# Cached attention gated by an MLP: how the last head group's sums, query and output matmuls are laid out in time

## The chip, the cores and the metric

One core of a Trainium2 chip. The number is device time in microseconds (us) of one execution of the whole kernel, as a median of several runs. TensorE (PE in the profile) multiplies matrices, VectorE (DVE) and ScalarE (ACT) work on tiles, GpSimd is POOL, and SyncE (SP) issues nearly all DMAs, in the order of the program.

## The reference

The inputs are bf16: x of 2048 x 512, a K and a V cache of 32 heads x 2048 keys x 128, and weights.

```python
xn = _layernorm(x)
q  = (xn @ wq) per head                       # 32 heads of 128
p  = softmax(q @ k.T * 128 ** -0.5)           # 2048 x 2048 per head
s  = concat(p @ v) @ wo                       # 2048 x 512
x1 = xn + shift(gelu(_layernorm(xn) @ w1)) @ w2   # shift: four quarters moved by 1, -1, 2, -2 rows
b  = x1 + gelu(_layernorm(x1) @ w3) @ w4
out = x + s * silu(b)
```

## The kernel before, in words

The kernel first makes xn, its transpose xnT and most of the MLP branch ("the start", up to about 130 us). Then comes the main loop over 128 **units**. A unit is one head for one tile of 512 queries. The heads go in eight groups of four (HG = 4, L51), and the order is group, query tile, head of the group (L120), so a group is 16 units, and the last group is units 112 to 127. A unit has eight **slots** (SPU, L54). Each slot takes two chunks of 128 keys.

In a slot TensorE makes two score matmuls into a PSUM tile ps_s (`s_slot`, L280; two such tiles exist, L95). ACT turns the tile into exponentials pT (L291). Some slots later TensorE multiplies two chunks of pT with V into ps_o (`pv_slot`, L310; two PSUM tiles, L92). How many slots later is PV's **lag**. `pv_run` (L648) sets it: 5 for the first eight units, then growing to 10, and 10 until unit PV1, from where it falls by one a unit to 5. Where it falls, the first slot of a unit holds four PV matmuls instead of two.

The softmax denominators are the column sums of pT over all keys. DVE adds the eight slots of pT into one tile acc (`add_first` L297, `add_next` L302, `add_last` L302, L307, L308). What is left is a sum over the 128 partitions, and there are two ways:

- `sums(u)` (L320): four small matmuls of TensorE, acc against a column of ones, into ps_sum, then the reciprocal rc on DVE (L327).
- `turn(u)` and `turned_sums(u)` (L331 to L342): a DMA transpose of acc on SP into tT, then a reduction on DVE (L338) and the reciprocal (L340). Units in the range TURN (L124) go this way: now 12 to 107.

In both ways rc goes to DRAM by one DMA (dr, L329 or L342) and comes back to all partitions by another (rb, `bcast`, L346). `norm(u)` (L358, DVE) multiplies ps_o by rb into oT, and thereby frees the PSUM tile of ps_o two units on.

When the four heads of a query tile are normalised, `norm_queue` (L662) puts four tiles of 128 rows into the queue wo_todo. `wo_slot` (L672) takes one: four matmuls (`wo_mm`, one for each head) into ps_wo, PSUM tag xm with one buffer, and then `wo_post` (L400), which on DVE adds ps_wo to the sums sacc (L416) or, in the last two groups, applies gate and input (L409 and L412, L409 and L397, or L425 and L427) and issues the output on SP.

The query tile of a unit takes four matmuls (`q_mm`, L264) and a copy (`q_copy`, L272). Units in the list `made` are made ahead in the start by `q_ahead` (L514): PSUM tag xa for even, xm for odd units, one buffer each, and the copy on ACT (L277). These are now 0 to 8, 112 to 116, 126 and 127, the last four of the list in the order 8, 116, 126, 127. All others are made in the loop in the unit before, in tag xa, with the copy on DVE (L275); ps_sum uses xa too.

The order of the instructions on each engine is the program's (`pin`, L62), written out by hand in the loop at L689 to L727: for each slot the scores, PV, query matmuls, then by slot number the sums, the normalisation, the Wo matmuls and the additions. For turned units a slot gets one query matmul (slots 7, 0, 1, 2) or one Wo matmul (slots 3 to 6). For others two query matmuls (slots 0, 1) and two Wo matmuls (slots 4, 5) share a slot, the sums are in slot 4, the normalisation in slot 3 (`late`, L710). The last unit, 127, is written out at L733 to L752; its own denominators and output come in the lines after.

Of the kernel before, what the change touches and what calls it, by code (L numbers as in the profile page):

```python
# [17 lines left out]
def kernel(  # L18
# [32 lines left out]
    HG = 4  # L51
# [69 lines left out]
    LATE = (QT - 2, QT - 1)  # L121
    GY = NG - 2
    NU = len(units)
    TURN = range(3 * HG, NU - 5 * HG)  # L124
    PV0, PV1 = 2 * HG, NU - 5 * HG + 3
    NS = NU * SPU
    kTs, vBs, wqs, wos, oTs, st = {}, {}, {}, {}, {}, {}
    todo = defaultdict(list)
# [49 lines left out]
    def stats(src, mv, rs, t):  # L178
        bn = smp.tile([P, nc.vector.BN_STATS_DIM], FP32, name="bn")
        pin(nc.vector.bn_stats(out=bn[:], in_=src))  # L180
        pin(nc.vector.bn_aggr(out=mv[:, t, :], in_=bn[:]))
        rsqrt(rs[:, t:t + 1], mv[:, t, 1:2])
# [34 lines left out]
    def m2(t):  # L217
        ps = psO.tile([P, D], FP32, tag="ps_o", name="ps_o")
        for jc in range(DC):
            c0 = BASE_J[jc] + t * P - SHIFT[jc]  # L220
            mm(ps[:], hT[:, jc, c0:c0 + P], w2_sb[:, jc, :], jc == 0, jc == DC - 1)
        return ps

    def x1(t, ps):
        pin(nc.vector.tensor_tensor(out=xall[:, t, :], in0=ps[:], in1=xall[:, t, :], op=ALU.add))
# [38 lines left out]
    def q_mm(u, dcs, tag="xa"):  # L264
        g, qt, hh = units[u]
        if dcs[0] == 0:
            st[u] = dict(psq=psX.tile([P, 512], FP32, tag=tag, name="ps_q"))
        for dc in dcs:
            mm(st[u]["psq"][:], wqs[g * HG + hh][:, dc, :],
               xnT[:, dc, qt * 512:(qt + 1) * 512], dc == 0, dc == DC - 1)  # L270
# [29 lines left out]
    def add_next(u, i):  # L300
        a = st[u]["acc"]
        pin(nc.vector.tensor_tensor(out=a[:], in0=a[:], in1=st[u]["pT"][i][:], op=ALU.add))  # L302

    def add_last(u):
        add_next(u, 3)
        a = st[u]["acc"]
        pin(nc.vector.tensor_tensor(out=a[:, 0:2, :], in0=a[:, 0:2, :], in1=a[:, 2:4, :], op=ALU.add))  # L307
        pin(nc.vector.tensor_tensor(out=a[:, 0, :], in0=a[:, 0, :], in1=a[:, 1, :], op=ALU.add))  # L308
# [40 lines left out]
    def norm(u):  # L349
        g, qt, hh = units[u]  # L350
        s = st.pop(u)
        if hh == 0:
            oTs[(g, qt)] = pB.tile([P, HG, 512], BF16, tag="oT", bufs=2, name="oT")
        o, rb, to = s["o"][:], s["rb"][:], oTs[(g, qt)][:, hh, :]
        if u in TURN:
            o = o.rearrange("k (j p) -> k p j", j=4)
            rb, to = (x.rearrange("k (p j) -> k p j", j=4) for x in (rb, to))
        pin(nc.vector.tensor_tensor(out=to, in0=o, in1=rb, op=ALU.mult))  # L358

    wo_box = {}  # L360
# [6 lines left out]
    def o_cols(g, qt, hh, ts):  # L367
        o = oTs[(g, qt)][:, hh, :]
        if (g * QT + qt) * HG + hh in TURN:
            return o.rearrange("k (p j) -> k j p", j=4)[:, ts, :]  # L370
        return o[:, ts * P:(ts + 1) * P]

    def wo_mm(g, t, hhs):
        if hhs[0] == 0:
            wo_box[0] = psX.tile([P, D], FP32, tag="xm", name="ps_wo")
        ts = t % 4
        for hh in hhs:
            mm(wo_box[0][:], o_cols(g, t // 4, hh, ts), wos[g * HG + hh][:], hh == 0, hh == HG - 1)
# [3 lines left out]
    def fin_load(t):  # L382
        xl = tokp.tile([P, D], BF16, tag="ta", bufs=10, name="xl")
        pin(nc.sync.dma_start(out=xl[:], in_=xsrc[t]))
        fin[t] = xl
# [14 lines left out]
    def wo_post(g, t, n):  # L400
        ps = wo_box.pop(0)
        if g == 0:
            sacc[t] = pS.tile([P, D], FP32, tag="sacc", bufs=NT, name="sacc")
            pin(nc.vector.tensor_copy(out=sacc[t][:], in_=ps[:]))
            return
        sa, gl = sacc[t][:], xall[:, t, :]
        if t // 4 in LATE and g >= GY:
            tm = pS.tile([P, D], FP32, tag="tm", bufs=4, name="tm")
            pin(nc.vector.scalar_tensor_tensor(  # L409
                out=tm[:], in0=ps[:], scalar=0.5, in1=gl, op0=ALU.mult, op1=ALU.mult))  # L410
            if g < NG - 1:
                pin(nc.vector.tensor_tensor(out=sa, in0=sa, in1=tm[:], op=ALU.add))  # L412
            else:
                y_out(t, tm, nc.sync)
            return
        pin(nc.vector.tensor_tensor(out=sa, in0=ps[:], in1=sa, op=ALU.add))  # L416
        if t // 4 in LATE and g == GY - 1:
            k = n + SPU * (t - 4 * LATE[0]) + 1
            at(max(k - SPU, n + 1), lambda: fin_load(t))
            at(k, lambda: y_scale(t))  # L420
            at(k + SPU, lambda: y_add(t))
        if g < NG - 1:
            return
        xl = fin.pop(t)
        pin(nc.vector.scalar_tensor_tensor(  # L425
            out=gl, in0=sa, scalar=0.5, in1=gl, op0=ALU.mult, op1=ALU.mult))
        pin(nc.vector.tensor_tensor(out=xl[:], in0=gl, in1=xl[:], op=ALU.add))  # L427
        pin(nc.sync.dma_start(out=out2d[t * P:(t + 1) * P, :], in_=xl[:]))
# [83 lines left out]
    made = []  # L512

    def q_ahead(u):  # L514
        q_mm(u, range(DC), ("xa", "xm")[u % 2])
        q_copy(u, nc.scalar)
        made.append(u)
# [24 lines left out]
        x1(t, ps)  # L542
    for t in range(4):
        stats(xall[:, t, :], mv2, rs2, t)
    for u in range(NU - 4 * HG, NU - 3 * HG):
        q_ahead(u)
    for t in range(4, 8):
        x1(t, m2(t))
# [2 lines left out]
    m1(1536, 512)  # L551
    for t in range(8, 11):
        x1(t, m2(t))
    for u in (2 * HG, NU - 12, NU - 2, NU - 1):
        q_ahead(u)
    for t in range(4, 8):
        stats(xall[:, t, :], mv2, rs2, t)
# [43 lines left out]
    pS = None  # L601
# [43 lines left out]
    wo_todo = deque()  # L645
# [16 lines left out]
    def norm_queue(u):  # L662
        norm(u)
        gg, qq, hh = units[u]
        if hh == HG - 1:
            wo_todo.extend((gg, 4 * qq + ts) for ts in range(4))
            if gg == NG - 1 and qq not in LATE:
                fin_load(4 * qq)

    UA, UB = NU - 2, NU - 1  # L670

    def wo_slot(part, n, each=2):  # L672
        gg, t = wo_todo[0]
        if part < HG // each:
            wo_mm(gg, t, tuple(range(part * each, (part + 1) * each)))
            return
        wo_todo.popleft()
        wo_post(gg, t, n)
        if gg == NG - 1 and t % 4 < 3 and t + 1 not in fin and t // 4 not in LATE:
            fin_load(t + 1)  # L680

    q_plan = defaultdict(list)
    for v in range(1, NU):
        if v not in made:
            for dc in range(DC):
                k = dc - 1 if v - 2 in TURN else dc // 2
                q_plan[(v - 1) * SPU + k].append((v, (dc,)))

    for n in range(UB * SPU):  # L689
        u, p = divmod(n, SPU)  # L690
        extra = len(wo_todo) > 3 and u < 2 * HG + 2 and pS is not None or u >= UA - 1
        s_slot(u, p)
        pv_run(n)
        for v, dcs in q_plan.get(n, ()):
            q_mm(v, dcs)
        if p == 0 and u - 2 in TURN:
            turned_sums(u - 2)
        if p == 1 and u - 2 in TURN:
            bcast(u - 2)
        if p == 0 and 1 <= u:  # L700
            add_last(u - 1)
        if p == 3 and u - 1 in TURN:
            turn(u - 1)
        if p == 0:
            twice = extra
        if twice and p < 3:
            wo_slot(p, n)
        if p == (3 if u - 1 in TURN else 2) and u + 1 not in made:
            q_copy(u + 1)
        late = 0 if u <= NU - 5 * HG else 2 if u <= NU - 5 * HG + 2 else 1  # L710
        if p == (7 if u - 2 in TURN else 2 + late) and 2 <= u:
            norm_queue(u - 2)
        if p == 3 + late and 1 <= u and u - 1 not in TURN:
            sums(u - 1)
        if p == 4 + late and 1 <= u and u - 1 not in TURN:
            bcast(u - 1)
        each, p0 = (1, 3) if u - 2 in TURN else (2, 4)
        if p0 <= p <= p0 + HG // each and wo_todo and pS is not None:
            wo_slot(p - p0, n, each=each)
        if p == 4:  # L720
            add_first(u)
        if p == 6:
            add_next(u, 2)
        held_mm(n)
        for fn in todo.pop(n, ()):
            fn()
        if n == HELD * SPU - 1:  # L727
            right.close()
            pS = right.enter_context(pool("pS", side="right", reuse_waits="tile"))
# [3 lines left out]
    n = UB * SPU  # L733
    ident2 = pS.tile([P, P], BF16, tag="ident2", name="ident2")
    pin(nc.vector.tensor_scalar(out=ident2[:], in0=ident[:], scalar1=2.0, scalar2=None, op0=ALU.mult))
    for p in range(SPU):
        s_slot(UB, p)
        pv_run(n + p)
        if p == 0:
            add_last(UA)  # L740
        if p < 2:
            wo_slot(p, n + p)
        if p == 3:
            norm(UB - 2)
            sums(UA)
            wo_slot(2, n + p)
        if p == 4:
            bcast(UA)
            add_first(UB)
        if p == 6:  # L750
            add_next(UB, 2)
# [90 lines left out]
```

## Time and profile before

| | |
|---|---|
| median of 3 runs | 1257.75 us (1257.68 to 1257.93) |
| profiled execution | 1258.32 us, its span 1256.5 |
| TensorE, large matmuls, start to start | 0.2158 us |
| units 96 to 107 (turned sums) | 8.63 us each |
| units 111 to 115 (sums by matmul, queries made ahead) | 8.39 to 8.40 |
| units 116 to 124 (sums by matmul, queries in the loop) | 8.80 each |
| unit 125, 126 (two Wo tiles each) | 9.02, 8.80 |
| exp of one slot (L291) on ACT | 1.02 us |
| last output landed | 1255.4 |

The span is what the profile shows of one execution, from its first to its last instruction. Durations are those of single instructions; an engine's next instruction can start before the end of the last, so a sum over a queue goes by the distances between starts. A unit's length is the distance between its first kT weight load and the next unit's.

### The profile page before, as it was taken

Reading aid. Unit: us, or ns where it says so; the run is one execution under the profiler, and the core shown is the slowest. Engines: PE = TensorE matmul, PEld = TensorE weight load, DVE = VectorE, ACT = ScalarE, POOL = GpSimd, SP = SyncE. Lnnn points to the kernel's source line nnn. Section 1 sums busy time; section 2 is a strip of 40 time slices with the busy share of each in tenths; the row PEclk is TensorE's granted clock in tenths of the full one; section 3 lists DMA queues with packets and bytes.
Section 4 is the critical chain, followed back from the end, with each engine's and each line's share of the span. In section 5 each row is a group of like instructions: output and inputs, shape, how many; then the busy total and the mean of one; then the engine's idle time right before and its main releaser. Section 6 shows DMA issues by size and latency. Waiting matters only on the chain.

```text
span 1256.5 us, 16202 instructions
## 1 busy us (share of the span) xinstructions
PE 1238.1 (99%) x5782; PEld 604.2 (48%) x5899; DVE 997.1 (79%) x1430; ACT 1100.6 (88%) x1113; POOL 34.4 (3%) x91
## 2 busy tenths in 40 slices
PE   8999999999999999999999999999999999999997
PEld 4444444444444444444444444444444444444443
DVE  7621567788888888888888888888888989978887
ACT  4344889999999999999999999999999999998886
POOL 4330000000000000000000000000000000000000
PEclk9999999999999999999999999999999999999999
DMA  6493011344345424454344514453355444452222
GB/s 157 104 167 77 10 32 46 79 91 96 58 74 108 107 51 75 97 102 84 60 89 98 110 42 86 87 118 68 56 101 104 100 67 84 97 94 51 68 56 59
DMA packets 224945, 103.86 MB, mean 83 GB/s; under 512 B 176928, under 2 KB 208160, under 8 KB 224864
## 3 DMA queue, kind: packets, MB, share of 16 engines
q1 hardware_dynamic: 221648, 100.07, 39.5%
q0 software_dynamic: 672, 1.84, 0.9%
q10 hardware_dynamic: 2544, 0.92, 0.3%
q8 instruction: 46, 0.75, 0.3%
q14 instruction: 35, 0.29, 0.1%
HBM read 67.90 MB, written 2.36 MB: 56 GB/s over the span
## 4 chain that ended last, share of the span: by engine, by line
PE 95%; DVE 2%; DMA 1%; ACT 1%; issue 1%; POOL 0%; SPq 0%; DVEq 0%; ACTq 0%
PE ps_s L109 39%; PE ps_o L109 36%; PE ps_q L109 9%; PE ps_wo L109 9%; PE ps_m L109 2%; DVE acc L302 0%; PE ps_sum L109 0%; ACT qT L277 0%; ACT xnT L199 0%; DMA rb<-dr 0%; DMA wq_e<-in_A_wq_dram 0%; DMA dr<-rc 0%; PE ps_w L109 0%; DMA xin<-in_A_x_dram 0%; DVE xall L425 0%
## 5 line engine op out<-in xcount | busy, mean ns | idle before, releaser
L291 ACT ACTIVATE pT<-ps_s 128x1024 bf16<-128x1024 f32 x1024 | 1034.6, 1023 | 76.0 <-PE ps_s L109 28.1
L109 PE MATMUL ps_s<-qT,kT 128*128 128x512 bf16 x2041 | 607.6, 379 | 0.6
L109 PE MATMUL ps_o<-pT,vb 128*128 128x512 bf16 x1962 | 589.0, 379 | 0.5
L302 DVE TENSOR_TENSOR acc<-acc,pT 128x2048 bf16<-128x2048 bf16 x255 | 309.3, 1213 | 98.2 <-ACT pT L291 95.7
L109 PEld LDWEIGHTS <-kT 128*128 128x128 bf16 x2048 | 231.1, 113 | 219.8 <-issue 0.8
L109 PEld LDWEIGHTS <-vb 128*128 128x128 bf16 x2048 | 200.3, 98 | 226.4 <-issue 0.3
L109 PE MATMUL ps_wo<-wo_h,oT 128*128 128x512 bf16 x492 | 177.9, 379 | 2.1
L297 DVE TENSOR_TENSOR acc<-pT 128x2048 bf16<-128x2048 bf16 x128 | 156.0, 1219 | 29.3 <-ACT pT L291 28.8
L109 PE MATMUL ps_q<-xnT,wq_h 128*128 128x512 bf16 x481 | 172.7, 379 | 2.1
L358 DVE TENSOR_TENSOR oT<-ps_o,rb 128x512 bf16<-128x512 f32 x127 | 86.9, 685 | 14.9 <-DMA rb<-dr 13.0
L307 DVE TENSOR_TENSOR acc<-acc 128x1024 bf16<-128x1024 bf16 x127 | 87.9, 692 | 4.3
L109 PEld LDWEIGHTS <-oT 128*128 128x128 bf16 x508 | 54.6, 110 | 56.6 <-DVE oT L358 1.2
L275 DVE CAST qT<-ps_q 128x512 bf16<-128x512 f32 x112 | 76.3, 682 | 0.3 <-PE ps_q L109 0.3
L109 PEld LDWEIGHTS <-wq_h 128*128 128x128 bf16 x484 | 47.2, 98 | 56.1 <-issue 0.2
L416 DVE TENSOR_TENSOR sacc<-ps_wo,sacc 128x512 f32<-128x512 f32 x96 | 65.5, 682 | 3.2 <-PE ps_wo L109 2.7
L338 DVE TENSOR_REDUCE sm<-tT 128x4 f32<-128x512 bf16 x96 | 64.9, 676 | 1.2 <-DMA tT<-acc 1.2
L308 DVE TENSOR_TENSOR acc<-acc 128x512 bf16<-128x512 bf16 x127 | 53.9, 425 | 4.3
L242 ACT ACTIVATE h2T<-ps_s 128x1024 bf16<-128x1024 f32 x28 | 28.7, 1024 | 24.0 <-PE ps_s L109 24.0
L109 PE MATMUL ps_s<-xn2T,w_sb 128*128 128x512 bf16 x219 | 48.6, 379 | 0.3
L109 PEld LDWEIGHTS <-w_sb 128*128 128x128 bf16 x304 | 29.7, 98 | 34.6 <-issue 2.1
L109 PEld LDWEIGHTS <-h2T 128*128 128x128 bf16 x224 | 21.5, 98 | 25.0 <-issue 0.2
L109 PE MATMUL ps_m<-w_sb,h2T 128*128 128x512 bf16 x106 | 31.0, 379 | 0.5
(73 smaller groups left out, 332.4 us busy)
## 6 DMA issues: line engine op xcount, KB each, us to landing
rb<-dr SPq DMA_DIRECT2D x127, 256.0 KB, 4.1
vb<-in_A_v_cache_dram SPq DMA_DIRECT2D x64, 256.0 KB, 3.2
wo_h<-in_A_wo_dram SPq DMA_DIRECT2D x32, 128.0 KB, 3.7
wq_h<-in_A_wq_dram SPq DMA_DIRECT2D x28, 128.0 KB, 3.2
w_sb<-in_B_w_dram SPq DMA_DIRECT2D x9, 256.0 KB, 4.8
kT<-in_A_k_cache_dram SPq DMA_TRANSPOSE x128, 3.2
xl<-in_A_x_dram SPq DMA_DIRECT2D x16, 128.0 KB, 3.6
dr<-rc SPq DMA_DIRECT2D x127, 2.0 KB, 1.4
```

Source lines behind the costliest of these rows:

```text
L109: pin(nc.tensor.matmul(out=out, lhsT=lhsT, rhs=rhs, start=start, stop=stop))
L242: pin(nc.scalar.activation(out=h2[c, f][:], in_=ps[:], func=ACT.Gelu_apprx_tanh))
L275: pin(nc.vector.tensor_copy(out=qT[:], in_=st[u].pop("psq")[:]))
L291: pin(nc.scalar.activation(out=s["pT"][-1][:, jj:jj + 2, :], in_=sps[:], func=ACT.Exp, scale=SCALE))
L297: pin(nc.vector.tensor_tensor(out=s["acc"][:], in0=s["pT"][0][:], in1=s["pT"][1][:], op=ALU.add))
L302: pin(nc.vector.tensor_tensor(out=a[:], in0=a[:], in1=st[u]["pT"][i][:], op=ALU.add))
L307: pin(nc.vector.tensor_tensor(out=a[:, 0:2, :], in0=a[:, 0:2, :], in1=a[:, 2:4, :], op=ALU.add))
L308: pin(nc.vector.tensor_tensor(out=a[:, 0, :], in0=a[:, 0, :], in1=a[:, 1, :], op=ALU.add))
L338: pin(nc.vector.tensor_reduce(out=sm[:], in_=s["tT"][:], axis=mybir.AxisListType.X, op=ALU.add))
L358: pin(nc.vector.tensor_tensor(out=to, in0=o, in1=rb, op=ALU.mult))
L416: pin(nc.vector.tensor_tensor(out=sa, in0=ps[:], in1=sa, op=ALU.add))
```

## The change

- TURN now ends at unit 115 instead of 107: units 108 to 115 get their sums by DMA transpose and reduction.
- PV's lag stays at 10 until unit 119 instead of 111, and then falls.
- From unit 14 on all query matmuls made in the loop come one to a slot (slots 7, 0, 1, 2).
- Units 118 to 127 get one Wo matmul to a slot (slots 4 to 7) and the result's reading on DVE in slot 0 of the next unit. In units 121, 126 and 127 a further tile goes into slots 1 and 2, two matmuls to a slot, read in slot 3. The sums move to slot 5, the normalisation to slot 4.
- For turned units the normalisation comes behind the Wo result in slot 7, not ahead of it.
- Made ahead are units 120 to 123 instead of 112 to 115, and 8, 127, 124 instead of 8, 116, 126, 127: 15 instead of 16.

```diff
-    TURN = range(3 * HG, NU - 5 * HG)
-    PV0, PV1 = 2 * HG, NU - 5 * HG + 3
+    TURN = range(3 * HG, NU - 3 * HG)
+    PV0, PV1 = 2 * HG, NU - 3 * HG + 3
...
-    for u in range(NU - 4 * HG, NU - 3 * HG):
+    for u in range(NU - 2 * HG, NU - HG):
         q_ahead(u)
...
-    for u in (2 * HG, NU - 12, NU - 2, NU - 1):
+    for u in (2 * HG, NU - 1, NU - HG):
         q_ahead(u)
...
-                k = dc - 1 if v - 2 in TURN else dc // 2
+                k = dc - 1 if v - 2 >= TURN.start else dc // 2
...
-        extra = len(wo_todo) > 3 and u < 2 * HG + 2 and pS is not None or u >= UA - 1
+        extra = len(wo_todo) > 3 and u < 2 * HG + 2 and pS is not None
+        if p == 0 and wo_box:
+            wo_slot(4, n, each=1)
         s_slot(u, p)
...
-        if p == (3 if u - 1 in TURN else 2) and u + 1 not in made:
+        if p == (3 if u - 1 >= TURN.start else 2) and u + 1 not in made:
             q_copy(u + 1)
-        late = 0 if u <= NU - 5 * HG else 2 if u <= NU - 5 * HG + 2 else 1
-        if p == (7 if u - 2 in TURN else 2 + late) and 2 <= u:
+        if u - 2 < TURN.start:
+            norm_p, sum_p, wo_p, each = 2, 3, 4, 2
+        elif u - 2 in TURN:
+            norm_p, sum_p, wo_p, each = 7, 5, 3, 1
+        else:
+            norm_p, sum_p, wo_p, each = 4, 5, 4, 1
+        if p == norm_p and 2 <= u and not u - 2 in TURN:
             norm_queue(u - 2)
-        if p == 3 + late and 1 <= u and u - 1 not in TURN:
+        if p == sum_p and 1 <= u and u - 1 not in TURN:
             sums(u - 1)
-        if p == 4 + late and 1 <= u and u - 1 not in TURN:
+        if p == sum_p + 1 and 1 <= u and u - 1 not in TURN:
             bcast(u - 1)
-        each, p0 = (1, 3) if u - 2 in TURN else (2, 4)
-        if p0 <= p <= p0 + HG // each and wo_todo and pS is not None:
-            wo_slot(p - p0, n, each=each)
+        if u in (NU - 7, UA) and p in (1, 2, 3):
+            wo_slot(p - 1, n)
+        if wo_p <= p <= wo_p + HG // each and wo_todo and pS is not None:
+            wo_slot(p - wo_p, n, each=each)
+        if p == norm_p and u - 2 in TURN:
+            norm_queue(u - 2)
...
         if p == 0:
+            wo_slot(4, n, each=1)
             add_last(UA)
-        if p < 2:
-            wo_slot(p, n + p)
+        if p in (1, 2, 3):
+            wo_slot(p - 1, n + p)
         if p == 3:
             norm(UB - 2)
             sums(UA)
-            wo_slot(2, n + p)
```

## The prediction

> **What bounds the kernel now.** I read the shares of busy time first, then TensorE's waits, then the windows, the timeline of the weight loads and the end of the chain of waits.
>
> ```profile
> PE 1238.1 (99%) x5782; PEld 604.2 (48%) x5899; DVE 997.1 (79%) x1430; ACT 1100.6 (88%) x1113; POOL 34.4 (3%) x91
> ```
>
> ```profile
> PE ps_q L109 <- ACT qT L277: 1.4, 2, 0.7
> PE ps_w L109 <- DVE oT L358: 0.7, 1, 0.7
> ```
>
> The first line is the page's, the other two are from the list of TensorE's waits (total us, times, longest). TensorE is never idle for long, so the time is its number of matmuls times their spacing, plus small holes. Every 512-column matmul of the main loop starts 0.2158 us after the one before it (40 in 8.63 us). The windows below are four stretches: a unit with transposed sums, a unit of the last head group with and one without its own query matmuls, and units 108 to 126 together.
>
> ```profile
> core 0: us, PE busy (x) PEld busy (x) DVE busy (x) ACT busy (x) POOL busy (x), PEclk, DMA share, GB/s
> 1018.05:1026.69 8.64, 8.59 (x41) 4.23 (x41) 7.76 (x12) 8.19 (x9) 0.00 (x0) 1.00 0.36 62
> 1164.19:1172.99 8.80, 8.75 (x45) 4.29 (x45) 7.77 (x12) 7.76 (x9) 0.00 (x0) 1.00 0.30 60
> 1112.60:1121.00 8.40, 8.35 (x42) 4.14 (x42) 6.65 (x10) 7.65 (x9) 0.00 (x0) 1.00 0.84 97
> 1069.85:1234.81 164.96, 163.98 (x807) 80.72 (x821) 143.07 (x201) 147.16 (x152) 0.00 (x0) 1.00 0.35 71
> ```
>
> The second unit has the same 40 large matmuls as the first, and takes 0.17 us more. Where that goes is in the timeline of the weight loads (start, length):
>
> ```profile
> 1164.19 0.37 PEld L109 LDWEIGHTS <-kT 128*128 128x128 bf16 x2
> ...
> 1165.52 0.33 PEld L109 LDWEIGHTS <-kT 128*128 128x128 bf16 x2
> ...
> 1166.82 0.33 PEld L109 LDWEIGHTS <-kT 128*128 128x128 bf16 x2
> ...
> 1168.54 0.33 PEld L109 LDWEIGHTS <-kT 128*128 128x128 bf16 x2
> 1168.97 0.31 PEld L109 LDWEIGHTS <-vb 128*128 128x128 bf16 x2
> 1169.40 0.40 PEld L109 LDWEIGHTS <-acc 128*128 128x128 bf16 x4
> ...
> 1169.97 0.33 PEld L109 LDWEIGHTS <-kT 128*128 128x128 bf16 x2
> ```
>
> A pair of kT loads opens a slot. The slot with the four small sum matmuls lasts 1.43 us (1168.54 to 1169.97), one with six large matmuls 1.30 (1165.52 to 1166.82): **a sum costs TensorE 0.13 us**. The pair that opens the unit takes 0.37 instead of 0.33: the score matmul waits 0.04 us for ACT to empty its PSUM tile, since two slots of four matmuls (1.73) lie before it, and a tile's round through matmul and exp needs 1.77 (0.63 from score matmul to exp, 1.02 exp, 0.05 to the next matmul, rows of the timeline, with some 0.06 more where the exp has further waits).
>
> **1. The queries made ahead.** Now four are made one after another (units 8, 116, 126, 127), three of them in PSUM tag xa; afterwards three (8, 127, 124) in xa, xm, xa.
>
> ```profile
> 45.30 1.03 PE L109 MATMUL ps_q<-xnT,wq_h 128*128 128x512 bf16 x4
> 47.02 1.02 PE L109 MATMUL ps_q<-xnT,wq_e 128*128 128x512 bf16 x4 [0.69 <-ACT qT L277]
> 48.72 1.89 PE L109 MATMUL ps_q<-xnT,wq_e 128*128 128x512 bf16 x8 [0.69 <-ACT qT L277]
> 50.45 4.64 PE L109 MATMUL ps_o<-w_sb,hT 128*128 128x512 bf16 x20
> 54.92 1.46 PE L109 MATMUL ps_s<-xn2T,w_sb 128*128 128x512 bf16 x6
> ```
>
> By start times each xa-after-xa step loses 47.02 - 45.30 - 0.86 = 0.85 us of TensorE to the copy at L277. In the new order unit 127 goes into the free tag, and unit 124 finds xa empty (copy ends 46.97) just as TensorE is free (47.03): both waits go, 1.70, and four matmuls leave this place, 0.86: the next matmuls could start at 47.89 instead of 50.45. Late next is DVE: its statistics of tiles 4 to 7 run until 49.31, then the addition L225 (0.69, now at 51.51, 1.06 after its matmuls began). The third of the five products must wait for it until 50.05 instead of 49.62; 0.08 of such waiting exists already, so 0.35 is given back. TensorE has no wait from 54.92 to the main loop; the transposed input landed by 48.5, and what is issued later is issued by engines that move along. **2.2 us saved**; bounds 1.7 (the two waits alone) and 2.56 (nothing given back).
>
> **2. The main loop, units 108 to 126.** Counting matmuls in issue order, these units have 749 large ones now: 161.63 us; 18 sums 2.34; of the 164.96 that leaves 0.99 of waits. After: 753 (one query more is made in the loop), 162.50; 10 sums, 1.30. The eight turned units pay instead a DMA transpose (3.8 us to landing, in units 12 to 107 beside other work) and a reduction on DVE (0.68 us). In the first window DVE has that reduction and is 7.76 of 8.64 busy with TensorE dense; so I cost it at nothing. If that cover went, a reduction (0.71 start to start) in eight units is 5.7.
>
> The row first, then the page: four loads and four one-column matmuls take 0.13. The Trainium skill ("TensorE: Matmul & The Clock Gate", LDWEIGHTS (loading the stationary operand)) gives a weight load as columns / 1.2 ns, 107 ns for 128; by an estimate from it four would take 0.43, eight units 3.4 instead of 1.04, and the whole change would save 2.4 us more. This case's trace has loads 28 to 36 ns apart there, so the measurement decides.
>
> Waits after: with five matmuls in a slot (1.08), two slots last 2.16 and no score matmul waits; slots without query or Wo matmuls remain three in a row in units 119, 120, 122 and 123, and cost as much as in 1112.60:1121.00, where the third costs 0.03: 0.14. New is a wait of PV. With lag 5 the PV of unit u opens its PSUM tile in slot 5, when the normalisation of u-2 (L358) has read it. Now that runs in slot 3; afterwards in slot 4, behind the output of a Wo tile that now ends in slot 7 and is read at the head of the unit. DVE, start to start from rows around 1206: the Wo result is ready 0.21 after the unit's first score matmul, L416 0.73, L425 0.73, L427 0.34, L302 1.26, L307 0.73, L308 0.34, query copy 0.60; L358 starts at 4.93 and ends at 5.61, PV wants 5.18 + 0.43 = 5.61, with 0.05 for the signal 0.05 late, in units 124 and 125; in 126, with two tiles, 0.10; in 123 perhaps 0.1, when the reciprocals of unit 121 come late behind the double tile of unit 121. Together 0.4 (bounds 0.14, only the old kind, and 1.0, as now). The loop: 162.50 + 1.30 + 0.4 = 164.2, **0.8 us saved** (1.0 to 0.2). In the turned units the normalisation also moves behind the Wo result on DVE, 0.6 later; PV needs it only 1.6 us after that, and TensorE does not wait.
>
> **3. The end.** Last to end is this chain:
>
> ```profile
> 1239.89 2.89 DMA dr<-rc
> ...
> 1242.79 3.31 DMA rb<-dr
> ...
> 1246.20 0.70 DVE oT L358
> ...
> 1246.94 2.78 PE ps_w L109 x12
> ```
>
> The reciprocal (L327) starts it at 1239.68, 4.62 after unit 127's first score matmul. Afterwards two Wo tiles are read on DVE ahead of it, in slots 0 and 3. Start to start: result ready 0.21, L409 0.72, L397 0.61, L302 1.26, L307 0.73, L308 0.34, L409 0.72, L397 0.61, L358 0.60: 5.80, so 1.18 later. On SP no output now stands between the two DMAs, and both outputs stand ahead. The pair of DMAs took 6.2 us here, 5.4 to 6.2 in the ten units before; with 5.6, as where an output was issued 0.7 us ahead (1223.70, 1231.96), the normalisation comes 0.6 later. TensorE waits for it, all behind it moves: **0.6 us lost** (0.35 to 1.2). DVE's additions for the late sums do not come later, since the second tile that now stands behind the reciprocal is gone from there.
>
> **The sum.** -2.2 - 0.8 + 0.6 = -2.4; I round towards the waits that I may have missed, -2.3. The profiled execution took 1258.32 (span 1256.5); it becomes 1256.0, and the median, 0.57 lower, **1255.5**. The bounds give 1258.32 - 0.57 - 3.2 = 1254.5 and 1257.1 (-2.56 - 1.0 + 0.35; -1.7 - 0.2 + 1.2).
>
> **Rivals.**
> - The late reciprocal at the end costs nothing, because its two DMAs land quicker with no output between them: for it, 1.38 us is the usual landing of the first; against it, the second was then 4.0 to 4.5. Saves 2.9: 1254.8.
> - The change does not do what it says: an even spread leaves the waits at 0.99, since PV's new wait replaces ACT's. Then -2.2 - 0.2 + 0.6 = -1.8, 1256.0, or 1256.4 where the end takes all 1.0.
> - The start's gain is lost: some load or transpose is due at a fixed time and TensorE waits for it instead. Against: no DMA wait of TensorE after 33.05. -0.2: 1257.6.
> - Slower: the broadcast rb lands after DVE wants it in units 123 to 126. The reciprocals now come about 5.7 after the unit's start and their broadcast lands 1.5 to 2.1 before its use; afterwards they come near 7.0, and L358 wants rb some 13.5 after: the pair of DMAs may last 6.4 before DVE waits, TensorE with it, in four units and at the end. In the last ten units it lasted at most 6.2, but 8.1 in unit 111, between K and V loads. At 7.5 it costs 5 x 1.1 = 5.5: 1261. It decides against the change from about 7.4 on.
>
> **Chances.** Forecast 0.58, quicker end 0.15, no evenness 0.12, start lost 0.08, slower 0.07. The bound of 0.2%, about what a measurement can tell, lies at 1255.23; a third of the forecast's cases (0.18) and the quicker end lie beyond it: faster 0.33, same 0.60, slower 0.07. The range 1254.4 to 1257.4 leaves out the lost start, the slower case and a few per cent of the others.
>
> **What would show it.** Right: the matmul after the queries starts near 47.9 and the next product near 52.7; units 108 to 116 last 8.63 each; no sums before unit 117; kT pairs of 0.33 in slot 0; reciprocal 5.8 after unit 127's start. Wrong: waits of L358 on rb or of PV on L358 beyond 0.3 us in units 118 to 126, TensorE waits between 55 and 130, or units 108 to 117 longer than 8.63, which would mean DVE lacks the room.

## The result and the profile after

The changed kernel takes 1255.22 us (median of 15 runs, 1254.90 to 1255.98) against 1257.87 for the kernel before (15 runs): the ratio is 0.9979, its 95% interval 0.9972 to 0.9986. That is 2.65 us less. It lies just beyond the 0.2% that the prediction took as its bound between same and faster, but the interval holds that bound (0.9980), so the runs do not settle on which side it is. The forecast was 1255.5.

Three stretches were forecast, and each can be cut out of the two traces by the start of a TensorE instruction. The stretch between the first two, from the MLP product to unit 108, is 1015.15 us in both.

| us | before | after | change | forecast |
|---|---|---|---|---|
| start: first query matmul of unit 8 to first matmul of the product ps_s<-xn2T | 9.62 | 7.40 | -2.22 | -2.2 |
| loop: first score matmul of unit 108 to that of unit 127 | 165.00 | 164.11 | -0.89 | -0.8 |
| end: from there to the span's end | 21.48 | 21.87 | +0.39 | +0.6 |

They add up to -2.72, where the medians give -2.65. The two profiled executions differ by less (span 1256.5 and 1254.2): in the one of after, the query matmuls begin 0.37 later (45.67 instead of 45.30), ahead of all that the change touches. In the eleven profiles of this document they begin anywhere from 44.96 to 46.59, so differences of a few tenths are read from the three stretches and not from the medians.

The start first, TensorE's rows of the timeline (start, length):

```profile
45.67 1.03 PE L109 MATMUL ps_q<-xnT,wq_h 128*128 128x512 bf16 x4
46.53 1.89 PE L109 MATMUL ps_q<-xnT,wq_e 128*128 128x512 bf16 x8
48.26 1.89 PE L109 MATMUL ps_o<-w_sb,hT 128*128 128x512 bf16 x8
50.40 2.83 PE L109 MATMUL ps_o<-w_sb,hT 128*128 128x512 bf16 x12 [0.25 <-DVE xall L225]
53.07 2.97 PE L109 MATMUL ps_s<-xn2T,w_sb 128*128 128x512 bf16 x13
```

The twelve query matmuls follow one another without the two waits of 0.69. The new wait is the one on DVE's addition (L225) that was forecast, after two of the five products. Less the 0.37, the products start at 47.89 and the next one at 52.70, as the prediction's signs have it (47.9, 52.7). Then the windows of unit 112 (now turned), of units 120 and 124, and of units 108 to 126:

```profile
core 0: us, PE busy (x) PEld busy (x) DVE busy (x) ACT busy (x) POOL busy (x), PEclk, DMA share, GB/s
1102.54:1111.17 8.63, 8.58 (x41) 4.22 (x41) 7.85 (x12) 8.18 (x9) 0.00 (x0) 1.00 0.48 113
1171.38:1179.76 8.38, 8.33 (x43) 4.17 (x43) 7.21 (x10) 7.79 (x9) 0.00 (x0) 1.00 0.25 63
...
1205.88:1214.68 8.80, 8.75 (x45) 4.30 (x45) 7.71 (x11) 8.08 (x9) 0.00 (x0) 1.00 0.23 61
1068.00:1232.12 164.12, 163.28 (x779) 80.63 (x794) 147.56 (x209) 153.32 (x153) 0.00 (x0) 1.00 0.34 77
```

Unit 112 has its reduction and its queries now and lasts 8.63, as the turned units before it; DVE is 7.85 busy in it, and TensorE has no hole. Over the whole stretch DVE works 147.56 us instead of 143.07. The weight loads of unit 126, slots 4 to 6, show the new wait of PV:

```profile
1227.58 0.33 PEld L109 LDWEIGHTS <-kT 128*128 128x128 bf16 x2
...
1228.66 0.33 PEld L109 LDWEIGHTS <-kT 128*128 128x128 bf16 x2
1229.09 0.10 PEld L109 LDWEIGHTS <-vb 128*128 128x128 bf16 x1
1229.40 0.10 PEld L109 LDWEIGHTS <-vb 128*128 128x128 bf16 x1 [0.21 <-issue]
1229.61 0.40 PEld L109 LDWEIGHTS <-acc 128*128 128x128 bf16 x4
...
1229.96 0.33 PEld L109 LDWEIGHTS <-kT 128*128 128x128 bf16 x2
```

```profile
1228.66 0.68 DVE L358 TENSOR_TENSOR oT<-ps_o,rb 128x512 bf16<-128x512 f32 x1
```

Two loads of V stand 0.31 apart instead of 0.216: PV waited 0.09 for the normalisation of unit 124 to free its PSUM tile. The row of the load names no releaser, but the normalisation (L358) ends at 1229.34, and PV starts at 1229.40. Slot 5 lasts 1.30 (1228.66 to 1229.96); 1.08 and a sum are 1.21. Last, the end of the chain of waits:

```profile
1237.52 0.68 DVE L358 TENSOR_TENSOR oT<-ps_o,rb 128x512 bf16<-128x512 f32 x1
1238.12 0.17 DVE L327 RECIPROCAL rc<-ps_sum 128x4 f32<-128x4 f32 x1
```

```profile
1238.31 1.39 DMA dr<-rc
...
1239.72 4.03 DMA rb<-dr
...
1243.84 0.70 DVE oT L358
...
1244.59 2.78 PE ps_w L109 x12
```

The first two rows are DVE's timeline, the others the chain. The reciprocal comes 5.79 us after unit 127's first score matmul (1232.33), 1.17 later than before. The two DMAs then take 5.44 instead of 6.2, and of the 1.17 the end feels 0.39.

### The profile page after: what moved, and what is told of

Its sections match the earlier page's. It is cut to its first block, busy times and chain, and to the rows that moved or that the text cites. A ratio compares the mean times of both kernels' runs of the same rounds, so it can differ in the third digit from the quotient of the medians.

```text
span 1254.2 us, 16153 instructions
## 1 busy us (share of the span) xinstructions
PE 1237.4 (99%) x5751; PEld 604.1 (48%) x5867; DVE 1001.4 (80%) x1439; ACT 1106.7 (88%) x1112; POOL 34.6 (3%) x91
## 3 DMA queue, kind: packets, MB, share of 16 engines
q0 software_dynamic: 672, 1.84, 0.8%
## 4 chain that ended last, share of the span: by engine, by line
PE 96%; DVE 1%; DMA 1%; issue 1%; ACT 1%; SPq 0%; DVEq 0%
PE ps_s L109 40%; PE ps_o L109 36%; PE ps_wo L109 9%; PE ps_q L109 9%; PE ps_m L109 2%; DMA w_sb<-in_B_w_dram 1%; DMA rb<-dr 0%; ACT xnT L199 0%; DVE y L397 0%; PE ps_sum L109 0%; PE ps_w L109 0%; ACT qT L277 0%; DVE bn L180 0%; DVE xall L225 0%; ACT hT L213 0%
## 5 line engine op out<-in xcount | busy, mean ns | idle before, releaser
L109 PE MATMUL ps_wo<-wo_h,oT 128*128 128x512 bf16 x495 | 184.0, 379 | 2.2
L109 PE MATMUL ps_q<-xnT,wq_h 128*128 128x512 bf16 x487 | 178.2, 379 | 2.3
L358 DVE TENSOR_TENSOR oT<-ps_o,rb 128x512 bf16<-128x512 f32 x127 | 86.6, 682 | 5.0 <-DMA rb<-dr 4.9
L338 DVE TENSOR_REDUCE sm<-tT 128x4 f32<-128x512 bf16 x104 | 70.3, 676 | 0.9 <-DMA tT<-acc 0.7
```

The source lines that it names most:

```text
L109: pin(nc.tensor.matmul(out=out, lhsT=lhsT, rhs=rhs, start=start, stop=stop))
L338: pin(nc.vector.tensor_reduce(out=sm[:], in_=s["tT"][:], axis=mybir.AxisListType.X, op=ALU.add))
```

## The experiments

Each was timed in turns with the kernel before on one chip, three chips over all (the kernel before took 1257.71, 1258.07 and 1258.32 on them); a ratio is to that kernel, with its 95% interval, and a distance to the changed kernel goes by way of it. Parts are cut out as in the table above. In two expectations "the page's price" is that of the Trainium skill which the prediction cites; "the third run" in two others is the one headed "The reciprocal first".

**The PSUM tags of the queries made ahead, alone**, in the kernel before:

```diff
-        q_mm(u, range(DC), ("xa", "xm")[u % 2])
+        q_mm(u, range(DC), ("xa", "xm")[len(made) % 2])
```

> The kernel before, and only the PSUM tags of the queries made ahead go by their place in the list instead of by the unit's number, so that units 8, 116, 126 and 127 use xa, xm, xa, xm. Nothing else changes; all sixteen queries are still made ahead. Theory: the two waits of 0.85 us for the copy go, the next products start at 48.75, after DVE's statistics have ended at 49.31 less the 1.06 that a product needs, so nothing is given back, and TensorE is dense from there to the end: 1.7 us faster than the kernel before. Rival (the start's gain is lost at a later fixed time): within 0.3 us of the kernel before.

Measured: 0.9986 (0.9977 to 0.9995), 1255.87 against 1257.71, 1.84 faster. The start is 7.92, 1.70 less, the loop 165.01 as before:

```profile
45.05 1.03 PE L109 MATMUL ps_q<-xnT,wq_h 128*128 128x512 bf16 x4
45.91 2.75 PE L109 MATMUL ps_q<-xnT,wq_e 128*128 128x512 bf16 x12
48.50 4.63 PE L109 MATMUL ps_o<-w_sb,hT 128*128 128x512 bf16 x20
52.98 3.40 PE L109 MATMUL ps_s<-xn2T,w_sb 128*128 128x512 bf16 x14
```

Sixteen query matmuls in a row, then the products in one row. The rival that a fixed time takes the gain back falls: what is saved near 50 us is there at the end.

**One of the two waits back**, in the changed kernel:

```diff
-    for u in (2 * HG, NU - 1, NU - HG):
+    for u in (2 * HG, NU - HG, NU - 1):
```

> The changed kernel, and only the order of the three queries is 8, 124, 127, in tags xa, xa, xm: one wait for the copy is back. Theory: that wait is 0.85 us of TensorE, but the next product then starts at 48.75 and DVE's 0.35 is not given back: 0.5 slower than the changed kernel, 2.15 faster than before. Rival (DVE gave nothing back): 0.85 slower than the changed kernel, 1.8 faster than before.

Measured: 0.9984 (0.9975 to 0.9993), 1256.31 against 1258.07. By medians it is 1.76 faster than before, which is nearer to the rival, and the interval holds both expectations (0.9983 and 0.9986). The trace tells them apart: the start is 7.91, 0.51 more than 7.40, with a wait of 0.69 (by starts 0.85) in it, and loop and end are as in the changed kernel (164.11 and 21.92).

```profile
45.50 1.03 PE L109 MATMUL ps_q<-xnT,wq_h 128*128 128x512 bf16 x4
47.21 1.89 PE L109 MATMUL ps_q<-xnT,wq_e 128*128 128x512 bf16 x8 [0.69 <-ACT qT L277]
48.94 4.64 PE L109 MATMUL ps_o<-w_sb,hT 128*128 128x512 bf16 x20
53.41 2.75 PE L109 MATMUL ps_s<-xn2T,w_sb 128*128 128x512 bf16 x12
```

The five products stand in one row again: DVE gives back 0.35 only when they begin before it is free.

**The sums issued three times**, in the kernel before, units 108 to 126:

```diff
-        for j in range(4):
-            mm(ps[:, j:j + 1], a[:, j, :], ones_t[:], True, True)
+        for _ in range(3 if u >= NU - 5 * HG else 1):
+            for j in range(4):
+                mm(ps[:, j:j + 1], a[:, j, :], ones_t[:], True, True)
```

> The kernel before, and the four small matmuls of each sum of units 108 to 126 are issued three times over (the same result is written again). Theory: 19 sums x 2 x 0.13 = 4.9 us slower than the kernel before. By the page's price of a weight load, 0.43 for a sum, 16 slower. Rival (the small matmuls hide beside the large ones and the sum's price is a wait that they share): under 2 slower.

Measured: 1.0036 (1.0023 to 1.0048), 4.56 slower. The loop grew by 4.55 for the 36 sums that units 109 to 126 have more: 0.126 each on average. In most of these units it is 0.27 for two; unit 125 grew by 0.03 alone, since it had a wait of 0.23 in slot 5 before (1.52 instead of 1.29), which the longer unit takes up. The nineteenth sum, in unit 127, brings the last reciprocal 0.27 later (4.89 instead of 4.62 after the unit's first score matmul), but in this execution the pair of DMAs behind it took 5.63 instead of 6.21, so the end is not longer (21.17). A sum costs TensorE 0.13, not 0.43; both rivals lie outside the interval.

**The turned units end at 107 again**, in the changed kernel:

```diff
-    TURN = range(3 * HG, NU - 3 * HG)
+    TURN = range(3 * HG, NU - 5 * HG)
```

> The changed kernel, and only the range of turned units ends at 107 again: units 108 to 115 get their sums by four small matmuls in slot 5, their normalisation in slot 4. Theory: 8 x 0.13 = 1.0 us slower than the changed kernel, so about 1.6 faster than the kernel before, with at most 0.3 of further waits. By the page's price of a weight load it would be 3.4 slower than the changed kernel, 0.8 slower than the kernel before. Rival (the transposes and the reductions on DVE cost as much as the matmuls): no slower than the changed kernel, 2.6 faster than before.

Measured: 0.9991 (0.9982 to 1.0000), 1256.60 against 1257.71, 1.1 faster than before and so 1.5 behind the changed kernel by medians. The interval leaves out the rival (0.9979) and the page's price (1.0006). The loop is 165.13, 1.02 more than 164.11: eight times 0.128. The other 0.3 lies at the end, where the last pair of DMAs took 5.8 us in this execution. Units 109 to 115 last 8.76 to 8.78 with the sums by matmul and 8.63 without: the transposes and reductions themselves cost the loop nothing.

**The query matmuls spread, alone**, in the kernel before:

```diff
-                k = dc - 1 if v - 2 in TURN else dc // 2
+                k = dc - 1 if v - 2 >= TURN.start else dc // 2
...
-        if p == (3 if u - 1 in TURN else 2) and u + 1 not in made:
+        if p == (3 if u - 1 >= TURN.start else 2) and u + 1 not in made:
```

> The kernel before, and only the query matmuls of the loop come one to a slot in the last head group too (slots 7, 0, 1, 2, copy in slot 3). Theory: slot 7 is no longer empty ahead of units 116 to 124, so the 0.04 us in slot 0 goes nine times: 0.36 faster than the kernel before, no other effect. Rival (the even spread does nothing, or ACT's rhythm gains more): no change, or over 0.8 faster.

Measured: 0.9997 (0.9988 to 1.0006), which is no difference by the runs. In the trace the loop is 164.67, 0.33 shorter: slot 0 of units 116 to 124 lasts 1.08 without a wait of its score matmul.

**The reciprocal first**, in the changed kernel, unit 127:

```diff
-        if p in (1, 2, 3):
+        if p in (1, 2):
             wo_slot(p - 1, n + p)
         if p == 3:
             norm(UB - 2)
             sums(UA)
+            wo_slot(2, n + p)
```

> The changed kernel, and only in unit 127 the second Wo tile is read on DVE behind normalisation and reciprocal instead of ahead of them. Theory: the reciprocal comes at about 4.6 instead of 5.8 after the unit's first score matmul; an output stands between the two DMAs again, which then last 5.4 to 6.2 instead of 5.4; the last normalisation comes 0.4 to 1.2 earlier and the end with it: 3.0 to 3.8 faster than the kernel before. Rival (the pair of DMAs stretches by what the reciprocal gains, or DVE's late additions become the bound): as the changed kernel, 2.6 faster than before.

Measured: 0.9973 (0.9963 to 0.9984), 1254.46 against 1257.71, 3.25 faster. The reciprocal comes at 4.62, the last normalisation at 10.42 instead of 11.51 after unit 127's first score matmul, and the end is 20.78 instead of 21.87: 1.09 of the 1.17 by which the reciprocal is earlier. By the runs alone the gain over the changed kernel is not shown (the interval holds its 2.65); the trace shows it. The chain does not pass through the DMAs any more:

```profile
1241.84 0.59 PE ps_o L109 x2
1242.43 0.45 PE ps_sum L109 x16
1242.88 0.45 PE ps_w L109 x2
...
1243.35 2.78 PE ps_w L109 x12
```

The last normalisation (1242.61, length 0.69) still waits 0.33 for its broadcast, but it ends at 1243.30, when TensorE comes free of its own work (1243.34): the two now end together, and a reciprocal earlier still would gain nothing more here.

**Wo two to a slot again**, in that kernel, units 118 to 126:

```diff
-            norm_p, sum_p, wo_p, each = 4, 5, 4, 1
+            norm_p, sum_p, wo_p, each = 3, 4, 4, 2
...
         if p == 0:
-            wo_slot(4, n, each=1)
             add_last(UA)
```

> The third run's kernel, and in units 118 to 126 the Wo matmuls come two to a slot again (slots 4 and 5), read in slot 6, with sums in slot 4 and the normalisation in slot 3. Theory: the 0.04 us of ACT in slot 0 is back in the seven units whose slots 6 and 7 are then empty (0.28), the waits of PV in units 124 to 126 (0.16) go: within 0.3 of the third run. Rival (one matmul to a slot is what shortens the loop): 0.5 to 1 slower than the third run.

Measured: 0.9972 (0.9960 to 0.9983), 1254.83 against 1258.07, 3.24 faster. The interval holds the rival too; the trace decides. The loop is 164.24 against 164.13 in the kernel it started from: 0.11 more. Slot 0 has its wait back (1.33 in units 119 to 123), slot 5 of units 124 to 126 has lost its own (1.29 in each, six matmuls), with the normalisation a slot earlier. For the Wo matmuls the even spread, with what moves along with it, is worth a tenth of a microsecond.

**Reciprocal first, and four queries made ahead**, in the kernel with the reciprocal first:

```diff
-    for u in (2 * HG, NU - 1, NU - HG):
+    for u in (2 * HG, NU - 1, NU - HG, NU - HG + 1):
```

> The changed kernel with the reciprocal of unit 126 first (as in the third run), and one query more made ahead: 8, 127, 124, 125 in xa, xm, xa, xm, so that unit 125's four matmuls leave the loop. Theory: at the start the next product begins 0.86 us later, at 48.75, where DVE no longer holds it back, so of the 2.2 saved there 1.7 stay; the loop loses four matmuls, 0.86: together 0.35 faster than the third run, 3.6 faster than the kernel before. Rival (work moved from one dense stretch of TensorE to another changes nothing, and DVE gave nothing back): as the third run, 3.25 faster than before.

Measured: 0.9971 (0.9959 to 0.9982), 1254.72 against 1258.07, 3.35 faster. Start 7.93 (0.53 more than in the run with the reciprocal first), loop 163.29 (0.84 less), end 20.88: a gain of 0.2 in the parts, which the runs do not separate from the one with the reciprocal first (3.25). The rival's half on DVE falls with the start: 0.53 more and not 0.86.

**A hop more for the reciprocals**, in the changed kernel, units 116 to 126:

```diff
         pin(nc.sync.dma_start(out=s["dr"][:], in_=rc[:]))
+        if u >= NU - 3 * HG:
+            dr2 = drp.tile([P, 4], FP32, name="dr2")
+            pin(nc.sync.dma_start(out=dr2[:], in_=s["dr"][:]))
+            s["dr"] = dr2
```

> The changed kernel, and the reciprocals of units 116 to 126 make one hop more in DRAM (a further 2 KB DMA on SP between dr and rb), so that the way from the reciprocal to the broadcast is one small DMA longer, 1.4 to 2.5 us. This tries the slower rival of the prediction: from what length of that way on does TensorE wait? In the changed kernel rb lands 0.7 to 1.7 us before its use in units 123 to 126. Theory: the longer way passes that room in part of the units; L358 comes late by 0.1 to 1.1 in units 123 to 126, TensorE waits in slot 5 by about as much (2 in all, 1 to 4), and the end moves by the whole hop (1.4 to 2.5): 3 to 6 slower than the changed kernel. Rival (only the end sees the broadcast, in the loop the two PSUM tiles of PV hide it): 1.4 to 2.5 slower than the changed kernel.

Measured: 1.0066 (1.0049 to 1.0083), 1266.84 against 1258.32: 8.5 us slower than the kernel before, so 11 slower than the changed kernel, nearly twice the upper end of what I had expected. Against the trace of the changed kernel 8.82 lie in the loop (172.93) and 1.53 in the end (23.40). The hop took 1.8 to 2.8 us, the whole way from the reciprocal's DMA to the landing 7.0 to 7.7; by the prediction's own price for its slower rival, five times what goes beyond 6.4, that is 3 to 6.5. The waits of the engines from 1140 us on (total us, times, longest), in which L362 is the normalisation:

```profile
DVE oT L362 <- DMA rb<-dr: 13.5, 8, 3.2
...
PE ps_o L109 <- DVE oT L362: 5.0, 6, 2.1
...
PE ps_w L109 <- DVE oT L362: 2.6, 1, 2.6
```

and DVE in unit 122:

```profile
1200.03 0.69 DVE L362 TENSOR_TENSOR oT<-ps_o,rb 128x512 bf16<-128x512 f32 x1 [1.96 <-DMA rb<-dr]
1200.64 1.22 DVE L297 TENSOR_TENSOR acc<-pT 128x2048 bf16<-128x2048 bf16 x1
1201.77 0.18 DVE L327 RECIPROCAL rc<-ps_sum 128x4 f32<-128x4 f32 x1
```

The next unit's reciprocal stands right behind the normalisation that waits for a broadcast, so lateness is handed from unit to unit: the reciprocals of units 117 to 120 come 7.4, 8.6, 9.7 and 11.9 us after the start of the next unit, where in the changed kernel they come 6.6, 6.4, 6.4 and 8.1 after it. DVE waits 1.1, 2.3 and 2.2 us for the broadcasts of units 116 to 118, where the long lag still hides it, and units 121, 122 and 123 then last 11.30, 10.30 and 12.40 instead of 9.19, 8.36 and 8.57. Not only units 123 to 126 pay, as I had it. Two of the three units pay by other ways too:

```profile
1184.06 0.59 PE L109 MATMUL ps_wo<-wo_h,oT 128*128 128x512 bf16 x2 [0.84 <-DVE sacc L420]
...
1190.47 0.43 DVE L431 TENSOR_TENSOR xl<-xall,xl 128x512 bf16<-128x512 bf16 x1 [1.63 <-DMA xl<-in_A_x_dram]
```

```profile
1210.14 0.81 PE L109 MATMUL ps_o<-pT,vb 128*128 128x512 bf16 x2 [2.05 <-DVE oT L362]
```

```profile
core 0: us, PE busy (x) PEld busy (x) DVE busy (x) ACT busy (x) POOL busy (x), PEclk, DMA share, GB/s
1210.10:1213.60 3.50, 3.46 (x13) 1.39 (x13) 2.43 (x3) 1.02 (x1) 0.00 (x0) 0.54 0.02 1
```

In unit 121 TensorE waits twice for the late DVE to read a Wo tile (1.66 of the 2.11, by starts). DVE then waits for an input tile, which SP loads behind the broadcast: with SP waiting for the hop, the load is issued at 1187.13 and lands at 1190.38. Only the last 0.45 is PV's wait for the normalisation. In unit 123 that wait is 2.21 by starts, and behind it the granted clock is 0.54 for 3.5 us, with matmuls 0.43 apart instead of 0.216: that is the other 1.6 of the 3.83. The shorter idle time in unit 122 (1.84 by starts) was not followed by a lower clock; from what length on it is, the runs do not show. The slower rival is real, and steeper than its price, since a late broadcast also holds up Wo tiles, the loads behind it on SP and, once, the clock: this was one small DMA away.

Not tried: PV's old lag with the new range of turned units. A turned unit is normalised in slot 7 of the second unit after it, now behind a Wo result whose matmuls stand in slots 3 to 6. With lag 5 PV would want the PSUM tile in slot 5 of the same unit, ahead of the last of these matmuls, and TensorE would wait for something that waits for TensorE. By this reading of the program the lag has no price of its own here; it is a condition. No run shows it.

## Why the prediction was right, point by point

- **The bound.** TensorE without holes: right. What the start saved was there at unit 108 in full (1015.15 us between the two in all eleven profiles, within 0.04).
- **Start, -2.2.** Right at -2.22, and by its own parts: two waits 1.70 (the run with tags alone), four matmuls 0.86, DVE's 0.35 given back (0.51 instead of 0.85 when a wait returns).
- **Sums, 8 x 0.13.** Right: 0.126 with more sums in the old kernel, 0.128 with eight put back in the new one. The 107 ns for a weight load (the Trainium skill, "TensorE: Matmul & The Clock Gate", LDWEIGHTS (loading the stationary operand)) agree with the length of a load in this trace (95 to 123 ns), but do not hold here as a price: the loads overlap, and a load and its one-column matmul take 32 ns of TensorE.
- **Turned sums at no cost.** Right: units 108 to 116 last 8.63 each.
- **Waits in the loop.** 0.31 are left (164.11 less 162.50 less 1.30), 0.4 was the value taken. Of the 0.7 that went, the queries' spread gave 0.33 and the Wo spread 0.11, each by a run (the second in the changed kernel); unit 125's wait of 0.23 in slot 5, which is gone from the trace of after, is about the rest, and no run tries it alone. The waits of PV in units 124, 125 and 126 were forecast as 0.05, 0.05 and 0.10 and are 0.03, 0.04 and 0.09; the 0.1 in unit 123 did not come: the double tile of unit 121 delayed unit 120's reciprocal, not unit 121's, and DVE's wait for it (0.22) lies in unit 122, where the lag is still 6.
- **The end, +0.6.** The reciprocal was right to 0.01 (5.80, measured 5.79). The pair of DMAs was taken at 5.6 and lasted 5.44, so this pair of profiles gives +0.39. In unit 126 it lasted 5.4 to 6.2 in the profiles of the runs without the hop, so the term has no sharper value: the old end is 21.48, 21.27 and 21.32 in three profiles (before and the runs with tags alone and queries spread), the new one 21.87, 21.92 and 22.19 (after, one wait back, turned to 107), by their means +0.64. The forecast of +0.6 holds better than the table shows, and that the table's three changes add up to the medians' difference is in part luck.
- **The last step of the sum.** -2.4 was rounded to -2.3 "towards the waits that I may have missed". The loop's waits came out smaller and not larger; without the rounding the forecast would be 1255.4.
- **The chances.** The result lies 0.01 us beyond the 1255.23 that was set as the bound between same and faster, where the forecast put a third of its own cases; "same" had the larger chance (0.60). The measurement cannot tell the two sides apart, so neither counts for or against the working.
- **The slower rival.** It did not come: in units 116 to 126 the pair of DMAs lasted 5.2 to 5.8, where it might take 6.4. Its mechanism is right, but its price of 1.1 for each of five places was too low, as the run with the hop shows.

## What to carry to other kernels

When one engine has no holes, count its instructions and price each kind by distances between starts in its own rows; three terms worked out so came within 0.2 us each out of 1258. Two producers in a row that share one PSUM buffer cost the whole copy each time (here 0.85 by starts): alternate the buffers by order of issue, not by a property of the work. What stands in front of an instruction that starts a DMA chain at the end is paid almost in full (here 1.09 of 1.17), as far as that chain ends last; move reads that nobody waits for behind it.

## What the runs showed of the hardware that was not expected

The small DMA and the broadcast behind it trade time with each other: in units 116 to 126 of the kernel before and of the changed one, where the first lands in 1.4 to 1.5 us the second takes 3.8 to 4.3, where it lands in 2.5 to 3.0 the second takes 3.2 to 3.5, so that the pair varies less (5.2 to 6.2) than its parts would let it. Why is open. A 2 KB copy from DRAM to DRAM took 1.8 to 2.8 us, where the same bytes from SBUF just ahead of it took 1.4 to 1.5 in nine of eleven cases (1.8 and 2.2 in the others). And a wait of 2.2 us on TensorE was followed by 3.5 us at a granted clock of 0.54 (unit 123 of the run with the hop), one of 1.84 us was not: here a wait cost more than its length.
